# A Fourier filter and a gated MLP on one core: another order in the filter stage, its last tile split over two engines

## The chip, the cores and the metric

The kernel runs on one core of a Trainium2 chip. Five engines work side by side: PE (matmuls), DVE and POOL (elementwise), ACT (activations and copies) and SP (here it issues transfers). The metric is the device time of one execution in microseconds. The kernel before has a median of 455.23 us over three runs (455.15 to 455.26).

## The reference, cut to what matters

`x` has 2048 rows of 512. Each row is normalised, the whole is taken through a 2-D Fourier transform, multiplied by a complex filter and transformed back; the result is added to `x`. Then a normalised copy goes through a gated MLP (512 to 1376 twice, GELU of one half times the other, back to 512) and is added again.

```python
def _A_ref(x, w_r, w_i):
    X = rfft2(x)                      # over 2048 rows and 512 columns
    return irfft2(X * (w_r + 1j * w_i), (S, D))

def _B_ref(x, w_gate, w_up, w_down):
    return (gelu(x @ w_gate) * (x @ w_up)) @ w_down

h = x + _A_ref(layernorm(x), A_w_r, A_w_i)
h2 = h + _B_ref(layernorm(h), B_w_gate, B_w_up, B_w_down)
```

All in float32.

## The kernel before, in words

The rows stand in 16 row blocks of 128 (index b), the 512 columns in four chunks of 128 or, in the Fourier domain, in 16 tiles (index t). Transforms are matmuls with tables of cosines. All results of a stage go back to one large tile in SBUF, `gh`. The eight banks of PSUM are the columns of `ps`.

The kernel has four stages.

1. *Transform over the rows* (to 32 us): per row block, statistics, folding on POOL, matmuls of line 288.
2. *The filter stage* (32 to 77 us), one pass over the 16 tiles t. Its order is written out by hand in the string `SECOND`, which is walked word by word; with `tc.manual_schedule` every engine gets its instructions in just that order. The words are:
   - `o3.0`: `over_d`, four matmuls of line 416 into two banks (the number behind the point is the first one), then two ACT copies into `dp` (line 420).
   - `f3`: `filtered`, two matmuls of line 427 into the two banks 4 and 5 (t even) or 6 and 7 (t odd); three products with the filter `wt` on DVE (lines 433, 434, 435) into `t1` and `t2`, which read these banks; the sum `z` on POOL (line 438) and a small addition of column 128 to column 0 (line 440). For the last tile, t = 15, sum and small addition are on DVE. `f` of tile t also issues on SP the load of the filter for tile t + 8 (line 202).
   - `b3`: `back`, four matmuls of line 448 that read `z` and fill bank t mod 2, then one ACT copy into `gh` (line 450).
   - `p3`: `patch_w`, a small ACT copy into the filter of tile t (line 453), which must come ahead of `f3`'s products and behind the load of this tile's filter.
   - `h`: one step in the preparation of the first and second weight tiles of the MLP ("raw tiles"): a rounded copy on ACT (line 93) and the remainder on POOL (line 94), and between the two tiles the transfer of the second (lines 131, 132) and four additions on POOL (lines 138 to 146).
3. *Transform back over the columns and rows, and the start of the MLP* (77 to about 131 us). Its order is the string `FIRST`. `U4.0` is `over_d_back` of row block 4 into bank 0: four matmuls of line 515, one for each chunk of columns, which read row block 4 of `gh` and so the back-transforms of all 16 tiles. `C4.0` copies the bank to a row on ACT (line 830), `V4.2` (DVE, line 838) and `X4` (POOL, line 866) unfold it, `M4.1` is the transform over the rows (PE, line 848), `H`, `G`, `I` the residual, `S`, `A`, `Q` statistics, and so on. `r0` to `r3` are the first four POOL steps on the third raw tile (`r0` is line 138), whose transfer is issued on SP ahead of `FIRST`.
4. *The MLP* (to the end), matmuls of lines 100 to 102 and 747.

A multiplication of float32 goes through PE in two passes, so four matmuls appear as eight in the trace. PE, ACT, DVE and POOL each work strictly in their own order: an instruction that waits holds all that stand behind it on its engine. SP's queue of transfers is in order too.

Of the kernel before, what the change touches and what calls it, by code (L numbers as in the profile page):

```python
# [20 lines left out]
P = 128  # L21
NB = 16
NT = 16
NF = 11
NQ = 260
# [6 lines left out]
BY_THEN = (8, 12, 9)  # L32

FIRST = """
U4.0 C4.0 r0 U0.1 C0.1 U1.2 U5.3 V4.2 X4 V0.3 C1.4 V1.0 C5.5 X0 M4.1 V5.1 X1 O4.0 X5 M0.2 H4 U2.3 O0.1 G4 I4
M5.1 C2.5 H0 V2.3 G0 S4 U7.2 M1.3 O5.0 A4 U6.0 I0 U3.4 X2 H5 C7.1 S0 O1.1 A0 H1 M2.1 C6.0 Q0 C3.5 E0.5 N0 G5
U12.3 R01 V7.4 I5 T01.2 G1 I1 V6.3 S5 X7 A5 R00 T00 S1 O2.1 M7.0 X6 s0.0 A1 a0 Q1 l0 V3.1 E1.6 c0 d0 f0 b0 U8.4
U9.7 N1 e0.1 m0 g0 H2 h0 R10 k0 T10 R11 H7 n0 T11.1 X3 a1 s1.2 b1 c1 i0 d1 j0 l1 M3.2 C8 S7 g0aP0 o0 M6.4 e1.0
h1 f1 U14.5 k1 C12 i1 m1 n1 O6.0 g1 g0ac1 U15.3 H3 j1 S3 C15 o1 A3 g0aP1 C9 A7 g0aP2 Q3 C14 G2 H6 g0ac2 E3.7 I2
N3 g0aP3 G6 U10.4 g0aP4 R31 S2 I6 R30 g0ad1 g0ac3 A2 S6 T31.5 A6 T30 s3.6 g0aP5 g1aP0 a3 Q2 E2.6 g0ady c3 C10  # L40
g0aP6 d3 b3 N2 f3 r1 g1ac1 g3 e3.4 K9.5 g1aP1 R20 r2 h3 g1aP2 i3 g1ad1 g1aP3 k3 R21 j3 T20 T21.7 g1ac2 a2 b2
s2.8 c2 g1aP4 g1ac3 l3 g1aP5 g0bP0 K12.4 d2 m3 g0ad2 n3 f2 g1ady g1aP6 e2.7 g2 g0bP1 o3 k2 l2 m2 g0bc1 h2 n2 i2
# [4 lines left out]
"""  # L47

SECOND = """
p0 p1 p2 h o0.0 h o1.6 o2.2 f0 o3.0 f1 p3 o4.2 f2 p4 h o5.0 o6.2 h f3 o7.0 h h p5 h f4 o8.2 p6 f5 b0 p7 b1 f6 o9.2 h h  # L50
h f7 p8 p9 b2 b3 o10.2 p10 f8 b4 h p11 o11.2 p12 f9 b5 o12.2 h h f10 b6 f11 o13.2 p13 b7 f12 h h o14.2 b8 f13 p14 o15.2
h f14 p15 b9 b10 h f15 b11 h b12 b13 b14 b15
"""
AHEAD = 8

# [2 lines left out]
def kernel(  # L58
# [47 lines left out]
    ps = ctx.enter_context(tc.tile_pool(name="ps", bufs=1, space=PSUM)).tile([P, 8, 512], F32, name="ps")  # L106
# [55 lines left out]
    with (  # L162
# [245 lines left out]
        w2 = ctx2.enter_context(tc.tile_pool(name="w2", bufs=2, reuse_waits="tile"))  # L408
        dps, zs = {}, {}
# [12 lines left out]
        def filtered(t):  # L422
            dp, wt = dps.pop(t), wts.pop(t)
            px = ps[:, 4 + 2 * (t % 2) : 6 + 2 * (t % 2), :NQ]
            for g in range(2):
                r = dp[:, g].rearrange("p e q -> p (e q)")
                pe.matmul(px[:, g], cfs[:, min(t, 1), g], r, start=True, stop=True)  # L427

            t1 = w2.tile([P, 2, NQ], F32, name="t1", bufs=3)
            t2 = w2.tile([P, 2, NQ], F32, name="t2", bufs=3)  # L430
            z = w2.tile([P, 2, NQ], F32, name="z", bufs=7)
            re, im = slice(0, 64), slice(64, P)
            dve.tensor_tensor(t1, px, wt[:, 0], op=ALU.mult)
            dve.scalar_tensor_tensor(t2[re], px[im], -1.0, wt[im, 1], op0=ALU.mult, op1=ALU.mult)
            dve.tensor_tensor(t2[im], px[re], wt[re, 1], op=ALU.mult)

            eng = dve if t == NT - 1 else pool
            eng.tensor_tensor(z, t1, t2, op=ALU.add)
            zs[t] = z
            eng.tensor_tensor(z[:, :, 0], z[:, :, 0], z[:, :, 128], op=ALU.add)  # L440

        def back(t):
            z = zs.pop(t)
            pg = ps[:, t % 2].rearrange("p (c g n) -> p c g n", c=4, g=2)
            for e in range(2):
                for g in range(2):
                    o, zg = pg[:, 2 * e : 2 * e + 2, g], z[:, g, 130 * e : 130 * e + P]
                    pe.matmul(o, zg, cis[:, min(t, 1), g], start=True, stop=True)  # L448
            ghv = gh.rearrange("p b (c t k) -> p t c b k", c=8, k=4)[:, t]
            act.activation(ghv, ps[:, t % 2].rearrange("p (c b k) -> p c b k", c=8, k=4), AF.Copy)  # L450

        def patch_w(t):
            act.activation(wts[t][:, :, :, 0:129:128], wh[:, t], AF.Copy)
# [2 lines left out]
        with tc.manual_schedule(engines={et.PE, et.Activation, et.DVE, et.Pool}):  # L456
# [50 lines left out]
        dve.bn_aggr(mv2[:, b], bn)  # L507
        yield

    def over_d_back(b, bank):  # L510

        g = gh[:, b].rearrange("p (c k) -> p c k", c=4)
        pv = ps[:, bank].rearrange("p (e s n) -> p e s n", e=2, s=2)
        for c in range(4):
            pe.matmul(pv[:, c // 2, (c + c // 2) % 2], g[:, c], dis[:, c], start=True, stop=True)  # L515

    def norm_scales(b, n):
# [269 lines left out]
    do = {}  # L787
# [25 lines left out]

    def whole(b):

        pv = sv = v = py = od = None
        xt, by_pe = sources[b], b in BY_PE

        def parts(a):
            return a.rearrange("p (e s n) -> p e s n", e=2, s=2)  # L820

        def back(k):
            nonlocal pv
            pv = ps[:, k]
            over_d_back(b, k)

        def keep(k):
            nonlocal sv
            sv = parts(rows[k])
            act.activation(rows[k], pv, AF.Copy)  # L830

        def unfold(k):
            nonlocal v
            v = rows[k]
            if b in BY_POOL:
                pool.tensor_tensor(parts(v)[:, :, 0], sv[:, :, 0], sv[:, :, 1], op=ALU.add)
            else:
                dve.tensor_tensor(parts(v)[:, :, 0], parts(pv)[:, :, 0], sv[:, :, 1], op=ALU.add)

        def back_s(k):  # L840
            nonlocal py
            py = ps[:, k].rearrange("p (e n) -> p e n", e=2)
            if by_pe:
                for e, m in enumerate((mis[:, b], nis[:, BY_PE.index(b)])):
                    pe.matmul(py[:, e], mis[:, b], v[:, :256], start=True, stop=False)  # L845
                    pe.matmul(py[:, e], m, v[:, 256:], start=False, stop=True)
            else:
                pe.matmul(ps[:, k], mis[:, b], v, start=True, stop=True)  # L848
# [12 lines left out]
        def unfold2(e, op):  # L861
            x2, h2 = (a.rearrange("p (e n) -> p e n", e=2) for a in (xt, gh[:, b]))
            return lambda: pool.tensor_tensor(h2[:, e], x2[:, e], od, op=op)

        do[f"U{b}"], do[f"C{b}"], do[f"V{b}"], do[f"M{b}"] = back, keep, unfold, back_s
        do[f"X{b}"] = lambda: pool.tensor_tensor(parts(v)[:, :, 1], sv[:, :, 0], sv[:, :, 1], op=ALU.subtract)
# [47 lines left out]
    for b in range(8):  # L914
        whole(b)
# [240 lines left out]
```

## Time and profile before

| What | us |
|---|---|
| Median of three runs | 455.23 |
| Profiled execution | 455.09 |
| Its span, first to last instruction | 453.3 |
| PE busy in the span | 438.1 |
| POOL busy | 276.0 |
| DVE busy | 276.7 |
| ACT busy | 206.5 |
| Filter stage on PE, first matmul of line 416 to first of line 515 | 32.40 to 76.89 |

The profile is of one execution. Its times run from the start of the span. "Idle before" is the time for which an engine had nothing to do ahead of an instruction, with the instruction that ended it. A group in the order of time has its start, its length and how many instructions it holds; matmuls overlap, so a group's row ends a little later than the next one starts.

### The profile page before, as it was taken

How to read it: one execution, taken by the hardware profiler on the slowest of the kernel's cores; microseconds unless marked ns; L12 is line 12 of the kernel's file. 1: busy time of each engine (PE TensorE's matmuls, PEld its weight loads, DVE VectorE, ACT ScalarE, POOL GpSimd, SP SyncE). 2: the span in 40 equal slices, each digit the busy share in tenths (PEclk: the TensorE clock that was granted, in tenths of full speed). 3: DMA queues.
4: the chain of work that ended last, by engine and by line, in shares of the span. 5: the costliest groups of instructions: out<-in, count | busy, mean ns of one | idle time of the engine just before them, and what ended most of it. 6: DMA issues, size and time to landing. Idle time of an engine off the chain costs nothing.

```text
span 453.3 us, 6435 instructions
## 1 busy us (share of the span) xinstructions
PE 438.1 (97%) x2289; PEld 371.2 (82%) x2289; DVE 276.7 (61%) x513; ACT 206.5 (46%) x433; POOL 276.0 (61%) x305
## 2 busy tenths in 40 slices
PE   3999999999999999999999999999999999999996
PEld 3999998788878777877888888888888888888875
DVE  5957886797565766358734579266655355635453
ACT  4979776688741243034322775242243024303420
POOL 6985996968869578738662643165566546663210
PEclk9999999999999999999999999999999999999999
DMA  8994805200032022112210213121122102210013
GB/s 293 392 395 145 274 11 185 95 25 1 25 116 74 31 83 93 48 46 71 69 46 25 70 40 123 48 93 46 26 69 71 46 24 71 69 46 25 23 70 117
DMA packets 21168, 41.05 MB, mean 91 GB/s; under 512 B 2064, under 2 KB 7696, under 8 KB 21008
## 3 DMA queue, kind: packets, MB, share of 16 engines
q1 hardware_dynamic: 20992, 40.51, 25.9%
q8 instruction: 18, 0.29, 0.3%
q10 hardware_dynamic: 144, 0.13, 0.1%
q14 instruction: 14, 0.11, 0.1%
HBM read 36.44 MB, written 4.19 MB: 90 GB/s over the span
## 4 chain that ended last, share of the span: by engine, by line
PE 93%; DVE 3%; ACT 2%; DMA 1%; issue 1%; SPq 0%; DVEq 0%
PE ps L747 26%; PE ps L100 15%; PE ps L102 15%; PE ps L101 15%; PE ps L288 5%; PE ps L416 3%; PE ps L515 3%; PE ps L427 3%; PE ps L448 2%; PE ps L848 1%; PE ps L956 1%; DMA gh<-in_x 1%; PE ps L554 1%; PE ps L548 1%; PE ps L845 0%
## 5 line engine op out<-in xcount | busy, mean ns | idle before, releaser
L100 PE MATMUL ps<-cb,gu 128*128 128x512 f32 (+1 forms) x336 | 127.8, 380 | 2.0 <-ACT s L651 1.6
L747 PE MATMUL ps<-wd,a 128*128 128x512 f32 (+1 forms) x537 | 125.9, 387 | 0.2 <-DVE gh L750 0.2
L102 PE MATMUL ps<-cb,gu 128*128 128x512 f32 (+1 forms) x336 | 124.8, 372 | 0.0
L101 PE MATMUL ps<-cb,gu 128*128 128x512 f32 (+1 forms) x336 | 124.8, 371 | 0.0
L747 PEld LDWEIGHTS ps<-wd,a 128*128 128x128 f32 x537 | 99.3, 188 | 22.0 <-DVE gh L957 1.0
L156 POOL TENSOR_TENSOR gu<-raw,gu 128x768 fp32r<-128x768 f32 (+1 forms) x54 | 78.3, 1479 | 39.8 <-DVE gu L153 36.0
L651 ACT ACTIVATE s<-ps 128x512 f32<-128x512 f32 (+1 forms) x72 | 40.4, 561 | 133.7 <-PE ps L102 133.4
L100 PEld LDWEIGHTS ps<-cb,gu 128*128 128x128 f32 x336 | 63.2, 188 | 14.9 <-ACT s L651 2.2
L101 PEld LDWEIGHTS ps<-cb,gu 128*128 128x128 f32 x336 | 63.3, 188 | 11.7 <-issue 1.0
L102 PEld LDWEIGHTS ps<-cb,gu 128*128 128x128 f32 x336 | 63.2, 188 | 11.0
L753 DVE TENSOR_TENSOR gh<-ps,gh 128x512 f32<-128x512 f32 x48 | 33.1, 691 | 53.4 <-PE ps L747 53.3
L496 POOL TENSOR_TENSOR wd<-wdr,wd 128x512 fp32r<-128x512 f32 x22 | 28.5, 1295 | 50.9 <-ACT wd L494 50.9
L660 DVE TENSOR_TENSOR ps<-ps,s 128x512 f32<-128x512 f32 (+1 forms) x48 | 31.0, 650 | 24.8 <-PE ps L102 22.5
L666 ACT ACTIVATE a<-ps 128x512 fp32r<-128x512 f32 (+1 forms) x48 | 26.9, 561 | 38.9 <-DVE ps L660 38.6
L138 POOL TENSOR_TENSOR raw<-raw 128x256 f32<-128x256 f32 x20 | 14.7, 737 | 38.3 <-DMA raw<-in_wgu 37.2
L673 DVE TENSOR_TENSOR a<-ps,a 128x512 fp32r<-128x512 f32 (+1 forms) x48 | 30.8, 641 | 11.5 <-ACT a L666 9.8
L654 DVE TENSOR_TENSOR s<-ps,s 128x512 f32<-128x512 f32 (+1 forms) x48 | 30.9, 643 | 10.3 <-PE ps L102 8.7
L657 ACT ACTIVATE s<-s 128x512 f32<-128x512 f32 (+1 forms) x48 | 28.2, 592 | 18.4 <-DVE s L654 18.4
L654 DVE TENSOR_TENSOR ps<-ps,s 128x512 f32<-128x512 f32 (+1 forms) x24 | 15.7, 654 | 27.7 <-ACT s L651 27.7
L288 PE MATMUL ps<-ms,pn 128*128 128x128 f32 x120 | 17.4, 295 | 7.6 <-ACT ms L256 7.4
L288 PEld LDWEIGHTS ps<-ms,pn 128*128 128x128 f32 x120 | 16.0, 209 | 8.0 <-POOL pn L263 7.4
L153 DVE CAST gu<-raw 128x1792 fp32r<-128x1792 f32 x18 | 19.6, 1091 | 4.5 <-PE ps L101 2.9
(124 smaller groups left out, 609.6 us busy)
## 6 DMA issues: line engine op xcount, KB each, us to landing
raw<-in_wgu SPq DMA_DIRECT2D x40, 256.0 KB, 3.1
wt<-in_w SPq DMA_DIRECT2D x16, 520.0 KB, 5.5
wdr<-in_wd SPq DMA_DIRECT2D x22, 256.0 KB, 2.7
out<-gh SPq DMA_DIRECT2D x15, 256.0 KB, 2.0
gh<-in_x SPq DMA_DIRECT2D x7, 512.0 KB, 8.0
row<-in_x SPq DMA_DIRECT2D x12, 256.0 KB, 3.0
mis<-in_mi SPq DMA_DIRECT2D x1, 1024.0 KB, 10.8
a<-in_x SPq DMA_DIRECT2D x4, 256.0 KB, 4.1
```

Of the source, the lines that this page charges most:

```text
L100: pe.matmul(o, lh, rh, start=(i == 0 and not onto), stop=False, skip_group_check=True)
L101: pe.matmul(o, lh, rl, start=False, stop=False, skip_group_check=True)
L102: last = pe.matmul(o, ll, rh, start=False, stop=(i == n - 1), skip_group_check=True)
L156: pooled["lo"] = pool.tensor_tensor(r[:, 1, m], t[:, m], r[:, 0, m].bitcast(F32), op=ALU.subtract)
L288: pe.matmul(pt[:, c], o, mc, start=(z == 0), stop=(z == len(parts[b][c]) - 1))
L496: pool.tensor_tensor(r[:, 1], t, r[:, 0].bitcast(F32), op=ALU.subtract)
L651: return lambda: act.activation(to, a, AF.Copy)
L654: return lambda: dve.tensor_tensor(to, a, b, op=ALU.add)
L660: return lambda: dve.tensor_tensor(u, u, g, op=ALU.mult)
L673: dve.tensor_tensor(a[:, 1], u, a[:, 0].bitcast(F32), op=ALU.subtract)
L747: pe.matmul(o, parts_of[tiles.index((q, f))][:, ha, i // 4, r], wds[f][:, hw, c], start=start, stop=stop)
L753: dve.tensor_tensor(gh[:, b, c], o, gh[:, b, c], op=ALU.add)
```

## The change

Five things change.

The string `SECOND` is another: the `h` and `p` steps, `o`, `f` and `b` stand in a different sequence. On PE, near the start of the filter stage, `f3` now comes ahead of `o6`. PE before (line 416 is `over_d`, 427 `filtered`, 448 or now 454 `back`):

```order
29 L416 MATMUL ps<-dfs,ts 128x130 x12
30 L427 MATMUL ps<-dp,cfs 128x260 x2
31 L416 MATMUL ps<-dfs,ts 128x130 x4
32 L427 MATMUL ps<-dp,cfs 128x260 x2
33 L416 MATMUL ps<-dfs,ts 128x130 x4
34 L427 MATMUL ps<-dp,cfs 128x260 x2
35 L416 MATMUL ps<-dfs,ts 128x130 x8
36 L427 MATMUL ps<-dp,cfs 128x260 x2
```

PE in the changed kernel, the same place:

```order
29 L416 MATMUL ps<-dfs,ts 128x130 x12
30 L427 MATMUL ps<-dp,cfs 128x260 x2
31 L416 MATMUL ps<-dfs,ts 128x130 x4
32 L427 MATMUL ps<-dp,cfs 128x260 x2
33 L416 MATMUL ps<-dfs,ts 128x130 x4
34 L427 MATMUL ps<-dp,cfs 128x260 x2
35 L416 MATMUL ps<-dfs,ts 128x130 x4
36 L427 MATMUL ps<-dp,cfs 128x260 x2
37 L416 MATMUL ps<-dfs,ts 128x130 x8
38 L427 MATMUL ps<-dp,cfs 128x260 x2
```

Row 36 of the new order is f3; it stood behind two `over_d` (x8) and stands behind one.

At the end of the filter stage PE had one `back` fewer behind f15. Before (f14, two backs, f15, five backs, then stage 3):

```order
62 L416 MATMUL ps<-dfs,ts 128x130 x4
63 L427 MATMUL ps<-dp,cfs 128x260 x2
64 L448 MATMUL ps<-cis,z 128x2x64 x8
65 L427 MATMUL ps<-dp,cfs 128x260 x2
66 L448 MATMUL ps<-cis,z 128x2x64 x20
67 L515 MATMUL ps<-dis,gh 128x128 x16
```

In the changed kernel:

```order
62 L416 MATMUL ps<-dfs,ts 128x130 x4
63 L427 MATMUL ps<-dp,cfs 128x260 x2
64 L454 MATMUL ps<-cis,z 128x2x64 x8
65 L427 MATMUL ps<-dp,cfs 128x260 x2
66 L454 MATMUL ps<-cis,z 128x2x64 x24
67 L524 MATMUL ps<-dis,gh 128x128 x16
```

f15 is followed by six backs (x24) where it was followed by five. The sixteen matmuls of the last row are U4, U0, U1 and U5 before, and u4, u0, w4, w0, U1 and U5 now.

POOL at the same place, with the third raw tile's first step (line 138) ahead of the unfolding of row block 4 (line 866). Before:

```order
72 L438 TENSOR_TENSOR z_814<-t1_812,t2_813 128x520
73 L440 TENSOR_TENSOR z_814<-z_814 128x2
74 L94 TENSOR_TENSOR gu_82<-raw_575,gu_82 128x256 x2
75 L138 TENSOR_TENSOR raw_913<-raw_913 128x256
76 L866 TENSOR_TENSOR row_889<-row_887 128x2x128
77 L866 TENSOR_TENSOR row_890<-row_888 128x2x128
```

In the changed kernel:

```order
73 L443 TENSOR_TENSOR z_812<-t1_810,t2_811 128x520
74 L444 TENSOR_TENSOR z_812<-z_812 128x2
75 L441 TENSOR_TENSOR z_832<-t1_830,t2_831 128x2x130
76 L94 TENSOR_TENSOR gu_82<-raw_574,gu_82 128x256
77 L881 TENSOR_TENSOR row_891<-row_889 128x2x128
78 L881 TENSOR_TENSOR row_892<-row_890 128x2x128
```

POOL has its half of the last z (line 441) ahead of the last split, and the raw step is gone from here; it now stands behind `C15` in `FIRST`.

The other four: `z` has 14 buffers instead of 7. The last `z` is added by halves of its columns, 0 to 129 on DVE and 130 to 259 on POOL. The last `back` fills two banks, columns by the first half of `z` into bank 1 and by the second into bank 3; ACT copies the first to `gh` and DVE the second. Row blocks 4 and 0 are begun by halves of d: `u4` and `u0` are the two chunks that the first copy fills, `w4` and `w0` the other two. And `r0` moves as said. On SP, the transfer of the second raw tile now stands one place earlier, ahead of the load of the filter for tile 13. Line numbers behind line 440 are 6 to 15 higher in the changed kernel.

The diff (of the two strings only the lines with a moved word that the text speaks of):

```diff
 FIRST = """
-U4.0 C4.0 r0 U0.1 C0.1 U1.2 U5.3 V4.2 X4 V0.3 C1.4 V1.0 C5.5 X0 M4.1 V5.1 X1 O4.0 X5 M0.2 H4 U2.3 O0.1 G4 I4
+u4.0 u0.1 w4 C4.0 w0 C0.1 U1.2 U5.3 V4.2 X4 V0.3 C1.4 V1.0 C5.5 X0 M4.1 V5.1 X1 O4.0 X5 M0.2 H4 U2.3 O0.1 G4 I4
...
-h1 f1 U14.5 k1 C12 i1 m1 n1 O6.0 g1 g0ac1 U15.3 H3 j1 S3 C15 o1 A3 g0aP1 C9 A7 g0aP2 Q3 C14 G2 H6 g0ac2 E3.7 I2
+h1 f1 U14.5 k1 C12 i1 m1 n1 O6.0 g1 g0ac1 U15.3 H3 j1 S3 C15 r0 o1 A3 g0aP1 C9 A7 g0aP2 Q3 C14 G2 H6 g0ac2 E3.7 I2
...
 SECOND = """
-p0 p1 p2 h o0.0 h o1.6 o2.2 f0 o3.0 f1 p3 o4.2 f2 p4 h o5.0 o6.2 h f3 o7.0 h h p5 h f4 o8.2 p6 f5 b0 p7 b1 f6 o9.2 h h
...
-h f14 p15 b9 b10 h f15 b11 h b12 b13 b14 b15
+h p0 h o0.6 o1.0 h o2.2 p1 h f0 o3.0 f1 p2 o4.2 f2 o5.0 p3 h f3 o6.2 p4 o7.0 h h p5 f4 p6 o8.2 p7 p8 f5 b0 b1 f6 h h
+o9.2 p9 h h p10 b2 f7 o10.2 f8 b3 o11.2 b4 p11 h h h f9 o12.2 p12 f10 h p13 b5 f11 o13.2 b6 p14 f12 p15 o14.2 h b7 f13
+h o15.2 f14 b8 b9 f15 b10 b11 h b12 b13 b14 b15
...
-            z = w2.tile([P, 2, NQ], F32, name="z", bufs=7)
+            z = w2.tile([P, 2, NQ], F32, name="z", bufs=14)
...
+            zs[t] = z
+            first = slice(0, NQ)
+            if t == NT - 1:
+                first, second = slice(0, 130), slice(130, NQ)
+                pool.tensor_tensor(z[:, :, second], t1[:, :, second], t2[:, :, second], op=ALU.add)
             eng = dve if t == NT - 1 else pool
-            eng.tensor_tensor(z, t1, t2, op=ALU.add)
-            zs[t] = z
+            eng.tensor_tensor(z[:, :, first], t1[:, :, first], t2[:, :, first], op=ALU.add)
             eng.tensor_tensor(z[:, :, 0], z[:, :, 0], z[:, :, 128], op=ALU.add)
 
         def back(t):
-            z = zs.pop(t)
-            pg = ps[:, t % 2].rearrange("p (c g n) -> p c g n", c=4, g=2)
+            z, last = zs.pop(t), t == NT - 1
+            ghv = gh.rearrange("p b (c t k) -> p t c b k", c=8, k=4)[:, t]
             for e in range(2):
+                pt = ps[:, 3 if last and e else t % 2]
+                pg = pt.rearrange("p (c g n) -> p c g n", c=4, g=2)
                 for g in range(2):
                     o, zg = pg[:, 2 * e : 2 * e + 2, g], z[:, g, 130 * e : 130 * e + P]
                     pe.matmul(o, zg, cis[:, min(t, 1), g], start=True, stop=True)
-            ghv = gh.rearrange("p b (c t k) -> p t c b k", c=8, k=4)[:, t]
-            act.activation(ghv, ps[:, t % 2].rearrange("p (c b k) -> p c b k", c=8, k=4), AF.Copy)
+                c = slice(4 * e, 4 * e + 4) if last else slice(0, 8)
+                if last and e:
+                    dve.tensor_copy(ghv[:, c], pt.rearrange("p (c b k) -> p c b k", c=8, k=4)[:, c])
+                elif last or e:
+                    act.activation(ghv[:, c], pt.rearrange("p (c b k) -> p c b k", c=8, k=4)[:, c], AF.Copy)
...
-    def over_d_back(b, bank):
+    def over_d_back(b, bank, cs=range(4)):
...
-        for c in range(4):
+        for c in cs:
...
+        def back_first(k):
+            nonlocal pv, bank
+            pv, bank = ps[:, k], k
+            over_d_back(b, k, (0, 1))
...
+        do[f"u{b}"], do[f"w{b}"] = back_first, lambda: over_d_back(b, bank, (2, 3))
```

More of the change, by code (lines that the diff above doesn't have):

```diff
@@ L49 @@
 SECOND = """
-p0 p1 p2 h o0.0 h o1.6 o2.2 f0 o3.0 f1 p3 o4.2 f2 p4 h o5.0 o6.2 h f3 o7.0 h h p5 h f4 o8.2 p6 f5 b0 p7 b1 f6 o9.2 h h
-h f7 p8 p9 b2 b3 o10.2 p10 f8 b4 h p11 o11.2 p12 f9 b5 o12.2 h h f10 b6 f11 o13.2 p13 b7 f12 h h o14.2 b8 f13 p14 o15.2
-h f14 p15 b9 b10 h f15 b11 h b12 b13 b14 b15
+h p0 h o0.6 o1.0 h o2.2 p1 h f0 o3.0 f1 p2 o4.2 f2 o5.0 p3 h f3 o6.2 p4 o7.0 h h p5 f4 p6 o8.2 p7 p8 f5 b0 b1 f6 h h
+o9.2 p9 h h p10 b2 f7 o10.2 f8 b3 o11.2 b4 p11 h h h f9 o12.2 p12 f10 h p13 b5 f11 o13.2 b6 p14 f12 p15 o14.2 h b7 f13
+h o15.2 f14 b8 b9 f15 b10 b11 h b12 b13 b14 b15
 """
@@ L814, in whole @@
     def whole(b):
-        pv = sv = v = py = od = None
+        pv = sv = v = py = od = bank = None
         xt, by_pe = sources[b], b in BY_PE
```

## The prediction

> **What bounds the kernel now.** I read four views in this order: the page's totals, the stretches with the busy time of each engine, the waits of PE, and the order of time around the one place where PE waits.
>
> The totals:
>
> ```profile
> span 453.3 us, 6435 instructions
> ...
> PE 438.1 (97%) x2289; PEld 371.2 (82%) x2289; DVE 276.7 (61%) x513; ACT 206.5 (46%) x433; POOL 276.0 (61%) x305
> ```
>
> PE is busy 97% of the span. The other engines count only where PE waits for them. The stretches (start:end, length, then busy time and instructions of PE, PEld, DVE, ACT, POOL, then PE's granted clock, 1.00) say where that is around the filter stage:
>
> ```profile
> 32.40:70.20 37.80, 37.80 (x278) 35.82 (x279) 30.61 (x44) 31.98 (x72) 30.47 (x43) 1.00 0.46 156
> 70.20:77.70 7.50, 6.38 (x51) 5.89 (x50) 4.46 (x7) 4.49 (x10) 4.55 (x7) 1.00 0.43 143
> ...
> 131.50:437.00 305.50, 305.37 (x1346) 249.47 (x1345) 172.46 (x284) 106.73 (x196) 172.34 (x171) 1.00 0.17 57
> ```
>
> From 32.40 to 70.20 PE has no idle time, so a new order of the same matmuls cannot shorten that piece; it can only open gaps in it. From 131.5 to 437 it has 0.13 us. In the 7.5 us between, at the end of the filter stage, it is idle 1.12 us. The waits of PE name the two causes (total, times, longest):
>
> ```profile
> PE ps L100 <- ACT s L651: 1.6, 3, 0.7
> ...
> PE ps L515 <- ACT gh L450: 0.7, 1, 0.7
> PE ps L448 <- DVE z L440: 0.4, 1, 0.4
> ```
>
> The last two are this place, the first lies behind 110 us. In order of time the place reads (start, length, engine, instruction, in brackets the idle time before):
>
> ```profile
> 45.93 1.95 PE L448 MATMUL ps<-cis,z 128*128 128x128 f32 x16
> 47.71 1.04 PE L427 MATMUL ps<-dp,cfs 128*128 128x260 f32 x4
> ...
> 69.91 1.04 PE L427 MATMUL ps<-dp,cfs 128*128 128x260 f32 x4
> 70.79 3.85 PE L448 MATMUL ps<-cis,z 128*128 128x128 f32 x32
> ...
> 71.16 0.70 DVE L433 TENSOR_TENSOR t<-ps,wt 128x520 f32<-128x520 f32 x1 [0.16 <-ACT gu L93]
> ...
> 71.88 0.60 ACT L450 ACTIVATE gh<-ps 128x512 f32<-128x512 f32 x1 [0.47 <-PE ps L448]
> 72.38 0.41 ACT L93 ACTIVATE gu<-raw 128x256 fp32r<-128x256 f32 x1
> 72.59 0.69 DVE L435 TENSOR_TENSOR t<-ps,wt 64x520 f32<-64x520 f32 x1
> ...
> 73.04 1.87 POOL L94 TENSOR_TENSOR gu<-raw,gu 128x256 fp32r<-128x256 f32 x2
> 73.31 1.01 DVE L438 TENSOR_TENSOR z<-t,t 128x520 f32<-128x520 f32 x1
> ...
> 74.36 0.57 DVE L440 TENSOR_TENSOR z<-z 128x2 f32<-128x2 f32 x1
> 74.68 0.60 ACT L450 ACTIVATE gh<-ps 128x512 f32<-128x512 f32 x1 [0.30 <-PE ps L448]
> ...
> 75.08 1.13 PE L448 MATMUL ps<-cis,z 128*128 128x128 f32 x8 [0.43 <-DVE z L440]
> ...
> 76.24 0.60 ACT L450 ACTIVATE gh<-ps 128x512 f32<-128x512 f32 x1 [0.96 <-PE ps L448]
> ...
> 76.89 1.16 PE L515 MATMUL ps<-dis,gh 128*128 128x128 f32 x8 [0.69 <-ACT gh L450]
> ```
>
> A back-transform of one tile (b, eight passes of L448) issues in 0.89 us: two start at 45.93 and the next work at 47.71. Five of them, b11 to b15, would take 5 x 0.89 = 4.45 us. They take 76.89 - 70.79 = 6.10 us. So the end of the stage loses **1.65 us**. That is the two idle times, 1.12 us, twice the 0.17 us by which the next group normally starts before the last one has drained (70.79 + 3.85 is 74.64, the issue would have been free near 74.48), and about 0.1 us slower issue behind each wait (1.13 and 1.16 us for eight where 1.05 is usual).
>
> **The change, part by part.**
>
> *The order of the filter stage.* No matmul is added or removed. f15 (the row at 69.91) now has five backs behind it ahead of b15, where it had four. It therefore starts 0.89 us sooner, at 69.02. From the end of its row DVE followed by 71.16 - 70.95 = 0.21 us; now that is 70.27, and three products with the row lengths above end 2.12 us later, near 72.4. The price is an early wait. f3 moves ahead of o6, to the place of o6 near 40.58, and must find its pair of banks released by the third product of f1:
>
> ```profile
> 39.64 1.99 PE L416 MATMUL ps<-dfs,ts 128*128 128x130 f32 x16
> 41.47 1.04 PE L427 MATMUL ps<-dp,cfs 128*128 128x260 f32 x4
> ...
> 45.02 1.07 PE L427 MATMUL ps<-dp,cfs 128*128 128x260 f32 x4
> ...
> 36.32 0.70 DVE L433 TENSOR_TENSOR t<-ps,wt 128x520 f32<-128x520 f32 x1 [6.87 <-issue]
> ...
> 39.90 0.69 DVE L435 TENSOR_TENSOR t<-ps,wt 64x520 f32<-64x520 f32 x1
> ...
> 44.20 0.69 DVE L435 TENSOR_TENSOR t<-ps,wt 64x520 f32<-64x520 f32 x1
> ```
>
> The product of f1 (39.90) ends at 40.59, so f3 waits some 0.06 us and pays 0.1 us for the slower issue: +0.16 us, with 0 and 0.4 as ends. f5 stays where it stood (45.02 in the old order) and needs the product that ends at 44.89, the last row: no wait.
>
> *The last z on two engines.* DVE adds 260 of 520 columns, POOL the rest. The nearest row for the DVE half is an addition of two SBUF operands of 256 columns; for the POOL half a row of the same size is the first of the second pair:
>
> ```profile
> 28.62 0.42 DVE L275 TENSOR_TENSOR us<-pn 128x256 f32<-128x256 f32 x1
> ...
> 98.92 0.73 POOL L573 TENSOR_TENSOR cb<-s,cb 128x256 fp32r<-128x256 f32 x1 [1.52 <-ACT cb L570]
> ```
>
> The DVE half lies between 0.42 and 1.01 us (the whole addition beside POOL). With L440's 0.57 us and two steps of 0.04 the first half is ready between 73.4 and 74.1 us. b15 can issue at 74.48 at the earliest, plus f3's 0.16: it is covered by 0.5 us or more, and the wait of 0.43 us goes. POOL's half must be there 0.45 us later. POOL's old queue shows L94 twice from 73.04; now the half stands ahead of one of them. A start at 72.9 and 0.73 us, or 0.94 as L94 took beside DVE, gives 73.6 to 73.8: covered by 1.3 us.
>
> Here a rule speaks against the change. The Trainium skill, "SBUF — State Buffer", section "Who interferes with whom", says that a DVE instruction with two SBUF inputs contends with a GpSimd instruction that reads SBUF, and that the one that comes second blocks for the whole instruction. The old rows look like it: 1.01 us for DVE and 0.94 each for POOL at 73 us. If DVE's half had to stand behind all of POOL's, the first half would be ready at 72.4 + 0.73 + 0.42 + 0.57 + 0.12 = 74.2 us, still ahead of 74.5, so by this rule the sum stays as it is.
>
> *The last back in two halves, copied by ACT and DVE; u and w.* Before, all eight passes, then one ACT copy of 0.60 us, then L515. Now the first four passes (0.45 us) fill one bank, ACT copies half of it while the other four run, and u4, u0 read only that half. Count from b15's start T: the fourth pass has drained at T + 0.61 (0.33 to its start, 0.28 for one pass). ACT is still at b14's copy until about T + 0.70 (that copy started 74.68 - 74.48 = 0.20 behind the free issue, and 71.88 to 72.38 shows that a copy frees ACT after 0.50). The half copy takes as long as the form of 256 columns:
>
> ```profile
> L93 ACT ACTIVATE gu<-raw 128x256 fp32r<-128x256 f32 x14 | 5.4, 408 | 0.1
> ```
>
> T + 1.11, and 0.05 to reach PE: u4 starts at T + 1.16 where PE would be free at T + 0.89. What is left is 0.27 us plus 0.1 for slow issue, **0.37 us**; the ends are 0.1 (ACT free in time) and 0.6 (the copy takes the full 0.60). The DVE copy of the other half starts with the last drain near T + 1.1, and with 0.42 to 0.60 us is done by T + 1.7; w4 comes behind u4 and u0, at T + 1.16 + 0.89 = T + 2.05. Covered by 0.3.
>
> C4 now stands behind u4, u0 and w4 instead of U4 alone. Its followers are POOL's X4 and PE's M4 (L848). In the old order POOL had the raw step r0 ahead of X4:
>
> ```profile
> 79.14 0.73 POOL L138 TENSOR_TENSOR raw<-raw 128x256 f32<-128x256 f32 x1 [4.23 <-DMA raw<-in_wgu]
> 79.82 2.80 POOL L866 TENSOR_TENSOR row<-row 128x256 f32<-128x256 f32 x4
> ...
> 80.61 1.99 PE L848 MATMUL ps<-row,mis 128*128 128x512 f32 x4
> ...
> 82.59 0.89 PE ps L515 x8
> ```
>
> X4 ended at 80.5 and M4 began at 80.61, hardly later than PE could. With r0 gone X4 starts with C4's end. C4 starts when w4 has drained, 3 x 0.45 - 0.11 + 0.28 + 0.04 = 1.56 us behind u4's start, takes 0.60, X4 0.73, the two steps 0.13: 3.0 us. M4's turn comes after four row blocks, 4 x 0.89 = 3.56 (last row). This fits by 0.5; with r0 still there (0.73) it would not. I take 0, with 0.2 as the bad end.
>
> *r0 moved back.* It now stands behind C15, ahead of the L573 at 98.92 above, where POOL was idle 1.52 us; its 0.73 us and its one read of a tile that has long landed fit. The two transfers of the third raw tile stay where they stand in SP's queue. Cost 0.
>
> *14 z buffers.* POOL no longer waits for a buffer. No PE wait in the old trace comes from that; gain 0.
>
> *The raw tiles' other steps* come sooner, and SP's load of the second raw tile now stands ahead of the load for tile 13, which is queued behind its wait for POOL:
>
> ```profile
> 49.68 0.38 SPq L131 DMA_DIRECT2D raw<-in_wgu  x1
> ...
> 51.41 2.48 SPq L202 DMA_DIRECT2D wt<-in_w  x2
> ...
> wt<-in_w SPq DMA_DIRECT2D x16, 520.0 KB, 5.5
> ```
>
> POOL's last step on the first raw tile follows its z3, whose inputs come at 44.89 (row above): 1.5 us for z3 and 1.4 for two splits give 47.8, two issues of 0.4, the load 5.5 us: tile 13 lands near 54.2. p13 stands on ACT ahead of o13's copy, near 58. Cost 0, with 4 us in hand.
>
> **Sum.** -1.65 + 0.37 + 0.16 = -1.12 us. Behind it PE, ACT, DVE and POOL all run on what PE releases, and the transfers of x and of the third raw tile are released by this same stretch, so the shift should last to the end. The profiled execution had 455.09 us, 1.79 beyond its span; it would have 453.97. The median of the runs is 0.14 higher, 455.23, so I predict **454.1 us**.
>
> **Rivals.**
>
> *DVE's pace opens gaps in the full stretch.* Between two f with one unit between them PE needs 0.88 + 0.89 = 1.77 us, DVE 3 x 0.715 = 2.15. Three places (f9 to f10, f10 to f11, f13 to f14) are like that; each can cost 0.38 us if DVE is then behind. For it: DVE is busy 30.6 of 37.8 us there. Against it, in the new order: DVE's nine products f0 to f8 end at 36.32 + 9 x 2.15 = 55.7 if nothing holds it; f9 stands twelve units behind f5, at 45.02 + 12 x 0.89 = 55.7, its products run from 56.95 to 59.1; f11, the first to ask for that pair of banks, comes at 55.7 + 2 x 1.77 = 59.24. It is close, 0.1 us. All three together give 1.14 us back: 455.2, no change. Chance 0.16.
>
> *The shift is lost behind 100 us.* PE's 1.6 us of waits for ACT (L651) would grow if ACT there hung on a transfer with a fixed time. Nothing in the waits names one. It would end at about 455.2. Chance 0.07.
>
> *Slower: tile 13 late.* If POOL finishes the first raw tile after about 52 us instead of 47.8, p13 holds ACT, o13's copy and then PE. Each us beyond costs PE one us; from 53.1 on the kernel is slower, and with POOL at 55, some 3 us late on PE, it ends at 456.1. Against it: POOL has gaps there. Chance 0.06. Other losses of that size, such as M4 or the second half late, together 0.05.
>
> *The end goes wholly.* If ACT is free in time and f3 does not wait, 0.1 stays: 453.7. Chance 0.06; the forecast itself 0.60.
>
> **How the numbers follow.** About 0.2%, 0.9 us, is what a measurement tells from no change, so 454.3 is the border, and the forecast lies 0.2 beyond it. Of its 0.60 I give 0.54 to faster and 0.06 to no difference (a residue at its upper end). With the 0.06 above faster has 0.60; no difference 0.06 + 0.16 + 0.07 = 0.29; slower 0.11. The range starts at 453.7 and reaches to 455.2, which takes in the rivals of no change.
>
> **What the profile will show.** PE's wait for z at the last back gone; the wait for ACT ahead of the first row block down from 0.7 to about 0.1 to 0.3 us; that block starting near 75.8 instead of 76.89; no DVE or POOL releaser for M4; p13 without a DMA wait; and all later PE times earlier by one same amount. I am wrong if the stretch 32.4 to 70 shows PE idle by more than 0.3 us, or the offset shrinks behind 100 us.

## The result and the profile after

The changed kernel has a median of 454.13 us over eight runs (453.98 to 454.49). The kernel before, run beside it on the same chip, has 455.19 us (455.06 to 456.76). The ratio is 0.9976 with a 95% interval of 0.9966 to 0.9985: faster by about 1.06 us. The forecast was 454.1 us. The profiled execution took 454.05 us.

The totals of the changed kernel:

```profile
span 452.3 us, 6433 instructions
...
PE 437.8 (97%) x2289; PEld 371.1 (82%) x2289; DVE 277.1 (61%) x514; ACT 205.6 (45%) x433; POOL 276.5 (61%) x306
```

The work is nearly the same: the span has lost 1.0 us, while PE is busy for 437.8 us where it was 438.1, ACT for 0.9 us less and DVE and POOL for 0.4 and 0.5 us more. The stretches of the changed kernel, with the same columns as in the prediction:

```profile
32.40:70.20 37.80, 37.80 (x275) 35.71 (x276) 31.39 (x45) 31.98 (x74) 31.51 (x44) 1.00 0.49 164
70.20:76.60 6.40, 6.33 (x55) 6.05 (x54) 3.67 (x6) 3.62 (x8) 3.96 (x7) 1.00 0.31 104
...
131.50:436.00 304.50, 304.33 (x1343) 249.09 (x1341) 172.75 (x283) 105.91 (x195) 171.86 (x171) 1.00 0.17 56
```

The full stretch is still full, although DVE and POOL have more to do in it. At the end of the filter stage PE is idle 0.07 us where it was 1.12. The waits of PE in the changed kernel (total, times, longest):

```profile
PE ps L288 <- ACT ms L256: 7.8, 2, 7.3
PE ps L100 <- ACT s L660: 1.6, 3, 0.6
PE ps L416 <- ACT ts L293: 0.7, 1, 0.7
PE ps L100 <- DVE ps L663: 0.3, 1, 0.3
PE ps L756 <- DVE gh L759: 0.2, 1, 0.2
```

The two rows of the kernel before for the end of the filter stage, 0.7 us for `gh` and 0.4 us for `z`, are gone, and no row for that place has come instead. The end of the stage in order of time, changed kernel:

```profile
69.06 1.04 PE L427 MATMUL ps<-dp,cfs 128*128 128x260 f32 x4
...
69.94 5.77 PE L454 MATMUL ps<-cis,z 128*128 128x128 f32 x48
...
70.31 0.70 DVE L433 TENSOR_TENSOR t<-ps,wt 128x520 f32<-128x520 f32 x1 [0.17 <-POOL z L443]
...
72.46 0.43 DVE L443 TENSOR_TENSOR z<-t,t 128x260 f32<-128x260 f32 x1
72.55 0.40 POOL L444 TENSOR_TENSOR z<-z 128x2 f32<-128x2 f32 x1
72.90 0.73 POOL L441 TENSOR_TENSOR z<-t,t 128x260 f32<-128x260 f32 x1
72.93 0.73 DVE L444 TENSOR_TENSOR z<-z 128x2 f32<-128x2 f32 x1
...
74.34 0.33 SPq L131 DMA_DIRECT2D raw<-in_wgu  x1
74.72 0.43 SPq L132 DMA_DIRECT2D raw<-in_wgu  x1
74.85 0.87 ACT L459 ACTIVATE gh<-ps 128x512 f32<-128x512 f32 x2 [0.42 <-PE ps L454]
75.26 2.49 SPq L792 DMA_DIRECT2D a<-in_x  x4
...
75.78 3.84 PE L524 MATMUL ps<-dis,gh 128*128 128x128 f32 x32
...
79.45 1.88 PE L862 MATMUL ps<-row,mis 128*128 128x512 f32 x4
```

L454 is the old L448, L524 the old L515, L862 the old L848. The 48 passes of b10 to b15 stand in one group, without a gap that the view shows, and the first row block follows 75.78 - 69.94 = 5.84 us after their start. Six backs at 0.89 us would take 5.34, so the end of the stage now loses **0.50 us**, where it lost 1.65.

Did the gain last to the end? The stage starts between 32.10 and 32.70 us in the profiles of this document, so distances are compared, not times. The rows for it are the first matmul group of the stage, the first matmul of the MLP and the last group of matmuls. Kernel before, order of time:

```profile
32.40 2.95 PE L416 MATMUL ps<-dfs,ts 128*128 128x130 f32 x24 [0.69 <-ACT ts L293]
...
96.64 0.47 PE L100 MATMUL ps<-cb,gu 128*128 128x256 f32 x1
...
437.08 12.68 PE L747 MATMUL ps<-wd,a 128*128 128x512 f32 x63 [0.17 <-DVE gh L750]
```

Changed kernel, order of time:

```profile
32.30 2.95 PE L416 MATMUL ps<-dfs,ts 128*128 128x130 f32 x24 [0.69 <-ACT ts L293]
...
95.57 0.47 PE L100 MATMUL ps<-cb,gu 128*128 128x256 f32 x1
...
436.05 12.68 PE L756 MATMUL ps<-wd,a 128*128 128x512 f32 x63 [0.17 <-DVE gh L759]
```

From the start of the stage, the first row block comes after 44.49 us before and 43.48 now (1.01 less), the MLP after 64.24 and 63.27 (0.97 less), the last group after 404.68 and 403.75 (0.93 less). What the end of the filter stage gained is kept almost whole.

### The profile page after: what moved, and what is told of

Read it like the earlier page. It is cut to its first block, busy times and chain, and to the rows that moved or that the text cites. A ratio compares the mean times of both kernels' runs of the same rounds, so it can differ in the third digit from the quotient of the medians.

```text
span 452.3 us, 6433 instructions
## 1 busy us (share of the span) xinstructions
PE 437.8 (97%) x2289; PEld 371.1 (82%) x2289; DVE 277.1 (61%) x514; ACT 205.6 (45%) x433; POOL 276.5 (61%) x306
## 4 chain that ended last, share of the span: by engine, by line
PE 90%; DVE 3%; ACT 2%; DMA 2%; POOL 1%; issue 1%; SPq 0%; POOLq 0%; DVEq 0%
PE ps L756 26%; PE ps L100 15%; PE ps L102 14%; PE ps L101 14%; PE ps L288 4%; PE ps L416 3%; PE ps L427 3%; PE ps L454 3%; PE ps L524 3%; PE ps L862 1%; PE ps L971 1%; DMA gh<-in_x 1%; POOL gu L156 1%; PE ps L563 1%; DMA raw<-in_wgu 1%; PE ps L557 1%
## 5 line engine op out<-in xcount | busy, mean ns | idle before, releaser
L100 PE MATMUL ps<-cb,gu 128*128 128x512 f32 (+1 forms) x336 | 127.9, 381 | 2.0 <-ACT s L660 1.6
L100 PEld LDWEIGHTS ps<-cb,gu 128*128 128x128 f32 x336 | 63.3, 188 | 14.9 <-ACT s L660 2.2
```

The costliest lines, as they stand in the source:

```text
L100: pe.matmul(o, lh, rh, start=(i == 0 and not onto), stop=False, skip_group_check=True)
```

## The experiments

The theory: the gain is the end of the filter stage, as the prediction summed it, and the order and the new tail (the sum on two engines, the halves of the last back, u and w) each carry a part. The rivals: one of the two carries all of it; or a part costed at nothing carries some.

Each group of kernels ran beside the kernel before on one chip; its median there was 455.17 us for the first four runs (order alone, without the order, r0, interleaved), 455.58 for the next four (whole row blocks, buffers, `z` on DVE, f3) and 455.39 for the last four (the two with x first, each with its kernel without it). The changed kernel itself was in none of these groups, so its median and theirs compare only by way of the kernel before. Below, "stage" is the distance from the first L416 group to the first row block, "to MLP" the distance from there to the first L100, both from the profiled execution.

| Kernel | median us (lowest to highest) | ratio to before, 95% | stage | to MLP |
|---|---|---|---|---|
| before | 455.19 | | 44.49 | 19.75 |
| after | 454.13 (453.98 to 454.49) | 0.9976 (0.9966 to 0.9985) | 43.48 | 19.79 |
| order alone | 454.71 (454.40 to 455.90) | 0.9993 (0.9985 to 1.0002) | 44.09 | 19.60 |
| without the order | 454.42 (454.13 to 456.93) | 0.9987 (0.9977 to 0.9998) | 43.25 | 20.41 |
| r0 at its old place | 455.44 (454.37 to 455.83) | 1.0001 (0.9993 to 1.0010) | 43.47 | 20.98 |
| row blocks whole | 454.28 (454.05 to 454.57) | 0.9965 (0.9950 to 0.9980) | 43.47 | 19.88 |
| 7 z buffers | 454.28 (454.13 to 454.48) | 0.9965 (0.9951 to 0.9980) | 43.47 | 19.79 |
| last z on DVE alone | 454.24 (454.03 to 454.58) | 0.9968 (0.9953 to 0.9983) | 43.47 | 19.79 |
| f3 behind o6 | 454.52 (454.38 to 454.91) | 0.9970 (0.9954 to 0.9985) | 43.83 | 19.81 |
| last two backs interleaved | 453.76 (453.48 to 455.14) | 0.9972 (0.9962 to 0.9981) | 43.24 | 19.51 |
| without the order, x first | 453.44 (453.24 to 453.77) | 0.9955 (0.9943 to 0.9967) | 43.26 | 19.60 |
| interleaved, x first | 453.46 (453.29 to 453.57) | 0.9955 (0.9942 to 0.9968) | 43.23 | 19.50 |

### The order alone

The kernel before with the new string `SECOND`, nothing else.

> The kernel before with the new string SECOND alone (one issue order for all engines in the filter stage; last z whole on DVE, last back whole, ACT copy whole, row blocks whole, r0 in its old place, 7 z buffers). My theory: the order removes the wait of PE for the last z (f15 starts 0.89 us sooner, z ready near 74.2 and needed near 74.4), and leaves the wait of 0.69 us for ACT ahead of L515, for 0.10 us paid at f3. The first L515 then starts near 76.2 to 76.3 against 76.89, total gain 0.6 us, about 454.6. Rival 1, the order carries all of the change: L515 near 75.8 and 454.1. Rival 2, the order is worth nothing since another wait takes over: L515 stays near 76.9, 455.2.

Measured: 454.71 us. Order of time, order alone:

```profile
69.87 5.76 PE L448 MATMUL ps<-cis,z 128*128 128x128 f32 x48
...
76.32 3.84 PE L515 MATMUL ps<-dis,gh 128*128 128x128 f32 x32 [0.69 <-ACT gh L450]
```

Six backs take 76.32 - 69.87 = 6.45 us, 1.11 more than 5.34. The wait for `z` is gone, the wait of 0.69 us for `gh` is still there in full. In the stage of this profile the order alone is worth 44.49 - 44.09 = 0.40 us; by the medians the gain is 0.46 us, where 0.6 was expected, and the interval of the ratio takes in no change. Between the theory and its second rival, then, the trace decides and not the time.

### Everything but the order

```diff
-h p0 h o0.6 o1.0 h o2.2 p1 h f0 o3.0 f1 p2 o4.2 f2 o5.0 p3 h f3 o6.2 p4 ...
+p0 p1 p2 h o0.0 h o1.6 o2.2 f0 o3.0 f1 p3 o4.2 f2 p4 h o5.0 o6.2 h f3 o7.0 ...
...
```

> The changed kernel with the old string SECOND: the split of the last z and of the last back, the half row blocks, r0 moved and 14 buffers stay, the order of the filter stage is that of before. My theory: DVE ends the third product of tile 15 near 73.3 as before, the half sum (0.43) and the small addition (0.73) bring the first half to 74.5, so PE waits about 0.1 us there (0.43 before) and then as in the changed kernel about 0.5 us in all ahead of the row blocks; no wait at f3. First row block near 75.9, total 454.2 to 454.3, a gain of 0.9 to 1.0. If the order were needed for the gain (rival), the wait for z stays near 0.4 and the total is 454.5 or more. If this theory holds, the two parts together are worth much less than the sum of each alone.

Measured: 454.42 us, a little above the expected range, and with a wide spread, though the first row block comes sooner than expected (75.45 us, not 75.9). The stage is shorter than in the changed kernel, 43.25 against 43.48 us: in the stage the tail alone gains 1.24 us, more than both together (1.01). PE's waits have no row for `z` although f15 has only four backs ahead of b15. What the kernel loses, it loses later. Order of time, without the order:

```profile
70.59 5.00 PE L454 MATMUL ps<-cis,z 128*128 128x128 f32 x40
...
73.58 0.57 DVE L444 TENSOR_TENSOR z<-z 128x2 f32<-128x2 f32 x1
...
74.09 0.74 POOL L441 TENSOR_TENSOR z<-t,t 128x260 f32<-128x260 f32 x1
...
75.54 0.33 SPq L131 DMA_DIRECT2D raw<-in_wgu  x1
75.91 0.44 SPq L132 DMA_DIRECT2D raw<-in_wgu  x1
76.46 1.82 SPq L792 DMA_DIRECT2D a<-in_x  x4
...
81.58 1.41 DVE L873 SCALAR_TENSOR_TENSOR a<-a,mv,ps 128x512 f32<-128x512 f32 x2 [1.13 <-DMA a<-in_x]
...
82.47 1.10 PE L862 MATMUL ps<-row,mis 128*128 128x512 f32 x2 [0.57 <-DVE a L873]
```

The wait for `z` goes by little. DVE's half is ready at 74.15 us and POOL's at 74.83, and PE is through with the issue of all five backs at 70.59 + 5.00 - 0.17 = 75.42, of which the four passes on POOL's half need 0.45.

The third raw tile is issued when POOL has done its last split of the second one. In the old order that is at 75.54 us, 1.20 us later than in the changed kernel (74.34), and the four loads of `x` stand behind it on SP. The residual of row block 4 (`H4`, L873) then waits for `x`, and PE behind it.

### Without the order, x ahead of the raw tile

The reading above was put to the test by one more edit in that kernel: the loads of `x` come first on SP, the third raw tile behind them.

```diff
-        nc.sync.dma_start(sources[b], x3[:, b])
+        i = nc.sync.dma_start(sources[b], x3[:, b])
+        loaded = i if b == 5 else b and loaded
...
-    next(raw2)
+    with tc.issue_after(loaded.ins):
+        next(raw2)
```

> The kernel with the new end and the old order (e2_tail), but with the four x loads (tiles a) issued on SP ahead of the third raw tile's two transfers, which wait for POOL's last split. My theory: in e2_tail the residual at 81.6 us waits for x because SP stood at the raw tile until 75.5 us, 1.2 us later than in the changed kernel; with x first the wait of PE for DVE's a (0.6 us) goes, and the time falls by about 0.5 us, from 454.4 to 453.9 or 454.0. Rival: the x loads themselves are not released before 75.5 us (their space is read until then), or the wait comes from elsewhere on DVE: then the wait stays and the time is 454.4.

The kernel without it ran again beside it:

> The new end with the old order once more, beside e10_x_first on the same chip, since the difference between them is only some 0.5 us. Both theories: about 454.4 us, with PE's wait for DVE's a of 0.5 to 0.6 us.

Measured: **453.44 us** with x first, 454.55 (453.54 to 455.72) without it. Order of time, with x first:

```profile
74.86 1.75 SPq L792 DMA_DIRECT2D a<-in_x  x4
76.71 0.38 SPq L131 DMA_DIRECT2D raw<-in_wgu  x1
...
80.62 1.60 DVE L874 SCALAR_TENSOR_TENSOR a<-a,mv,ps 128x512 f32<-128x512 f32 x2 [0.15 <-ACT od L868]
```

The residual no longer waits for a transfer, and PE no longer for the residual. This confirms the cause; the gain is 1.1 us, twice what was expected. The spread suggests why: without the edit twelve executions lie 2.2 us apart, with it five lie 0.5 us apart. The second profile without it is of the fastest execution (453.54 us): there the way to the MLP is 19.73 us, the residual waits 0.45 us for `x`, and PE has no such wait. In the first profile the residual waited 1.13 us, PE 0.57, and the way was 20.41 us. So the time at which `x` lands changes from one execution to the next, and a profile of one execution shows one draw of it.

This kernel is 0.7 us faster than the changed one by their medians; the two ran in different groups, and their ratios to the kernel before are 0.9955 (0.9943 to 0.9967) and 0.9976 (0.9966 to 0.9985). So the new order is not needed for the gain. It has two effects: in the stage it costs 43.48 - 43.26 = 0.22 us once the new tail is there, and it lets POOL finish the second raw tile 1.2 us sooner, which brings the loads of `x` forward. The second can be had by four transfers in another place.

### r0 at its old place

```diff
-u4.0 u0.1 w4 C4.0 w0 C0.1 U1.2 ...
+u4.0 u0.1 w4 C4.0 r0 w0 C0.1 U1.2 ...
...
-... C15 r0 o1 ...
+... C15 o1 ...
```

> The changed kernel with r0 back behind C4, ahead of X4 on POOL. My theory: r0 waits for the third raw tile, whose transfer was issued 0.6 us sooner than in the kernel before, so r0 runs from about 78.55 to 79.28 instead of not at all, X4 ends near 80.0 and M4 (L862) starts near 80.05 instead of 79.45: 0.4 to 0.6 us of the gain is lost, 454.6. Rival, the move is worth nothing (M4 has 0.5 us in hand or the later work takes it up): M4 at 79.5 and 454.1.

Measured: 455.44 us, the same as the kernel before (ratio 1.0001). The loss is 1.3 us where 0.4 to 0.6 was expected. Order of time, r0 at its old place:

```profile
74.56 1.65 SPq L132 DMA_DIRECT2D raw<-in_wgu  x1
...
79.05 0.73 POOL L138 TENSOR_TENSOR raw<-raw 128x256 f32<-128x256 f32 x1 [4.89 <-DMA raw<-in_wgu]
79.74 2.78 POOL L881 TENSOR_TENSOR row<-row 128x256 f32<-128x256 f32 x4
...
80.51 1.98 PE L862 MATMUL ps<-row,mis 128*128 128x512 f32 x4 [0.92 <-POOL row L881]
```

The stage still gains its 1.02 us, and all of it is given back within 5 us: POOL stands at the raw tile until it lands, X4 comes behind, and the first L862 waits 0.92 us. That r0 at this place takes the gain is shown; how late the tile lands is not the same in all kernels. The order alone has r0 at its old place too, and there the tile lands 1.5 us sooner:

```profile
77.54 0.73 POOL L138 TENSOR_TENSOR raw<-raw 128x256 f32<-128x256 f32 x1 [3.86 <-DMA raw<-in_wgu]
```

X4 follows at 78.23 us, and PE has no wait at the first L848. The raw tile's first transfer was issued at 73.70 us there and at 74.19 here: POOL's last split, which releases it, comes later here because POOL adds its half of `z` ahead of it. The other 1.0 us of the 1.5 is open. The issue of L132 took 1.65 us here, against 0.43 in the changed kernel and in the order alone, and the times spread over 1.5 us, so the transfer may have had a bad draw; no run shows how much of the median that is.

### Three parts, one at a time

Three parts were undone one at a time in the changed kernel: the row blocks begun whole (`U4.0 C4.0 U0.1 C0.1` in place of the halves), seven buffers for `z`, and the last `z` added by DVE alone.

> The changed kernel with row blocks 4 and 0 begun whole again (U4, C4, U0, C0 instead of u4, u0, w4, C4, w0, C0), all else kept. U4's first two chunks read what ACT copied, its third what DVE copies until 76.23. My theory: PE comes to the third chunk at 75.78 + 0.45 = 76.23 and so waits about 0.05 us and pays 0.1 for the slower issue: the halves are worth 0.1 to 0.2 us, total 454.2 to 454.3. Rival, the halves carry the gain at this place: a wait of 0.4 us or more ahead of the third chunk, 454.5 or more. Rival, they are worth nothing, since C4 and X4 start sooner with U4 whole: 454.1.

> The changed kernel with 7 z buffers. My theory: no tile is more than six ahead of its back, so seven buffers hold it, no wait changes on PE, 454.1. Rival, POOL's sums wait for the backs that free their buffers and the last sums come late: a wait of PE for z appears, 454.4 or more.

> The changed kernel with the last z whole on DVE as before (the back and its copies still in halves). My theory: with the new order the whole sum (1.01 us beside POOL) and the small addition (0.57) end near 74.1, b15 needs it at 74.38, so nothing changes, 454.1; the split over two engines is covered twice. Rival, the shared port makes DVE's whole sum longer than in the kernel before, and PE waits at b15 by 0.2 to 0.5 us, 454.3 to 454.6.

Measured: 454.28, 454.28 and 454.24 us. All three stages are 43.47 us long, as in the changed kernel (43.48). With whole row blocks the way to the MLP is 0.09 us longer, too little to tell from the times; buffers and the split leave nothing to see. Given the new order, then, the sum on two engines is worth nothing; given the new tail, the order is worth nothing inside the stage. They are two cures for one wait of 0.43 us. That it is the sum on two engines that cures it in the tail is read from the rows (DVE's addition takes 0.43 us where it took 1.01); no run had that sum alone in the old order.

### f3 behind o6 again

```diff
-... p3 h f3 o6.2 p4 ...
+... p3 h o6.2 f3 p4 ...
```

> The changed kernel with f3 behind o6 again, where it stood before; all else kept. By the term of my prediction f3's early place costs 0.1 us (its row is 1.15 instead of 1.04 us long), so this would give 454.0. Rival: ACT has p3 and one split ahead of o6's copies in the new order, so o7, which needs the banks of o5, comes to PE before ACT has read them, and PE waits 0.2 to 0.4 us at o7 instead: 454.3 to 454.5.

Measured: 454.52 us, the stage 43.83 - 43.48 = 0.35 us longer. Order of time, f3 behind o6:

```profile
39.62 2.44 ACT L420 ACTIVATE dp<-ps 64x520 f32<-64x520 f32 x4
...
40.88 1.16 PE L416 MATMUL ps<-dfs,ts 128*128 128x130 f32 x8 [0.21 <-ACT dp L420]
```

Changed kernel, the same place:

```profile
40.55 1.15 PE L427 MATMUL ps<-dp,cfs 128*128 128x260 f32 x4
41.53 1.95 PE L416 MATMUL ps<-dfs,ts 128*128 128x130 f32 x16
```

In the new order o6 comes directly behind o5 if f3 does not stand between them, and it asks for the banks of o4. ACT comes to its copies of o4 and o5 only at 39.62, four of them in a row, and o6 waits for the first two. With f3 ahead of o6 they have time. So the theory, a gain of 0.1 us, was wrong. The rival had the loss right, but at the tile behind: it is o6 that waits for the banks of o4, not o7 for those of o5. f3 itself takes 41.53 - 40.55 = 0.98 us in the changed kernel, where 0.88 is usual.

### The last two backs interleaved

In the changed kernel ACT has to copy all of b14 before it can copy the first half of b15, and PE waits for both. Here b14 and b15 run as four half backs, the first halves of both ahead of the second ones, in four banks; ACT copies the first halves, DVE the second.

```diff
-... b12 b13 b14 b15
+... b12 b13 x14 x15 y14 y15
...
-def back(t):
+def back(t, es=(0, 1)):
...
-                pt = ps[:, 3 if last and e else t % 2]
+                pt = ps[:, ((0, 2), (4, 3))[t - NT + 2][e] if last else t % 2]
```

> The changed kernel with the last two backs interleaved: first halves of b14 and b15, then second halves, first halves copied by ACT and second halves by DVE, into four different banks. The 0.45 us of matmuls more between the first half of b15 and u4 should cover the rest of the copy chain. My theory: the 0.5 us that the changed kernel still loses between the last back (48 passes from 69.94, issue free at 75.28) and the first row block (75.78) goes but for 0.1; row block near 75.3 to 75.4, total 453.7. It needs the last z 0.45 us sooner (at 73.95; it was ready at 73.66). Rival 1: the wait is not that chain but a cost of changing the line, and 75.8 stays, 454.1. Rival 2: z comes too late by the added DVE work, and PE waits at b15 instead, 454.1 or more.

Measured: 453.76 us. Order of time, interleaved:

```profile
70.06 5.76 PE L454 MATMUL ps<-cis,z 128*128 128x128 f32 x48
...
75.66 3.74 PE L526 MATMUL ps<-dis,gh 128*128 128x128 f32 x32
```

5.60 us for six backs: 0.26 lost instead of 0.50. The half that is gone, 0.24 us, was PE's wait for ACT's copies. The half that is left is not that chain. ACT copies each back as soon as its last pass is through, so the starts of the copies show where PE comes late. Changed kernel, b10 to b13:

```profile
71.03 0.60 ACT L459 ACTIVATE gh<-ps 128x512 f32<-128x512 f32 x1 [0.78 <-PE ps L454]
71.93 0.60 ACT L459 ACTIVATE gh<-ps 128x512 f32<-128x512 f32 x1 [0.29 <-PE ps L454]
...
72.94 0.60 ACT L459 ACTIVATE gh<-ps 128x512 f32<-128x512 f32 x1
73.83 0.60 ACT L459 ACTIVATE gh<-ps 128x512 f32<-128x512 f32 x1 [0.30 <-PE ps L454]
```

The copy of b14 follows at 74.85. The steps are 0.90, 1.01, 0.89 and 1.02 us: b12 and b14 each come 0.12 us late. The interleaved kernel has the same step at b12 (72.05 to 73.06). The kernel before has it at b13:

```profile
72.77 0.60 ACT L450 ACTIVATE gh<-ps 128x512 f32<-128x512 f32 x1
73.79 0.60 ACT L450 ACTIVATE gh<-ps 128x512 f32<-128x512 f32 x1 [0.42 <-PE ps L448]
```

The views name no releaser for it. The time met the expected 453.7 us in part by luck: the stage gained 0.24 us where 0.4 was expected, and 0.28 us came behind it, on the way to the MLP (19.51 against 19.79), which the expectation did not speak of.

Then both improvements together, with this kernel again beside it on the same chip:

> The changed kernel with its last two backs interleaved by halves (e8_inter), and x ahead of the third raw tile. In e8_inter DVE's residual at 80.8 us still waited 0.24 us for x. If that is on PE's path, 453.5 to 453.6; if SP's order costs nothing once POOL is done by 74.3 us, 453.76 as before, within 0.1.

> The interleaved end once more, beside e11_inter_x_first on the same chip. Both theories: 453.7 to 453.8 us.

Measured: 453.46 us (453.29 to 453.57) with x first, 453.81 (453.61 to 454.02) without. x first is worth 0.35 us here. Together they are no faster than x first in the old order (453.44). By their medians both beat the changed kernel, and clearly the one before.

## Why the prediction was right

The time came out within 0.1 us of the forecast, and the mechanism is the one that was forecast. In the stage the sum is 0.11 us off (1.01 us measured, 1.12 forecast), by one term. What the prediction missed is how the parts hang on each other, and it was lucky with one of them, r0.

**The place.** It was the end of the filter stage and nothing else: PE's idle time there fell from 1.12 to 0.07 us, the stage is 1.01 us shorter, and 0.93 us of that is there at the last group of matmuls. Forecast: 1.12.

**The wait for z.** Forecast: f15 at 69.02, DVE's first product at 70.27, the first half of `z` ready at 73.4 to 74.1, POOL's half at 73.6 to 73.8. Measured: 69.06, 70.31, 72.93 + 0.73 = 73.66, and 72.90 + 0.73 = 73.63. But the prediction treated order and split as one cure. The runs show that the order alone and the tail alone each remove the wait.

**The residue.** The steps behind b15's start T held. The 48 passes free the issue at 69.94 + 5.77 - 0.17 = 75.54 us, so T is 75.54 - 0.89 = 74.65. ACT starts the copy of b14 at 74.85, T + 0.20 as forecast, and ends the half copy at 74.85 + 0.87 = 75.72; u4 starts at 75.78, T + 1.13, where T + 1.16 was forecast. The wait behind the free issue is 0.24 us against 0.27. The mis-sized step is T: "b15 can issue at 74.48 at the earliest, plus f3's 0.16" is 42.24 us behind the start of the stage, and b15 came at 74.65 - 32.30 = 42.35, 0.11 late. Backs in a row do not all issue in 0.89 us: one of the five in the kernel before and two of the six now take some 0.12 us more. The old trace had it already, since 70.79 + 4 x 0.89 is 74.35 and not 74.48. In the working of the 1.65 us this does not show, because the slow issue behind the second wait was counted in it, and that row (1.16) lies beyond 76.89, where the 1.65 end.

**f3.** Forecast 0.16 us, measured 0.1 at f3 itself. f15 comes 36.76 us behind the start of the stage where 69.02 - 32.40 = 36.62 would be free of any price, so all prices ahead of it are 0.14 us together. The size is right, but f3's place was costed against its old place in the old order. In the new order the old place costs 0.35 us more. The prediction did not look at what o5 and o6 in a row would ask of ACT there.

**r0.** Its move was costed at 0, and with that the sum came out. The sentence "with r0 still there (0.73) it would not" is right, but its working implies only 3.0 + 0.73 - 3.56 = 0.17 us. Put back, r0 takes the whole gain: 0.92 us at L862 in the profile, 1.3 us in the median. The step that was missing is r0's wait for its transfer, which is released by POOL's last split and not by PE. As far as this working goes, it is luck that the move was part of the change.

**The transfers.** "The transfers of x and of the third raw tile are released by this same stretch" is right, and it rests on the order: with the old one POOL is 1.2 us later with the second raw tile, and `x` behind it is late. So what the order costs in the stage it more than gives back on SP, which the prediction did not see.

**What was weighed against it.** DVE's half of `z` came first (72.46) and took 0.43 us, so it was not held up. Who came second was: POOL's addition of two columns, 0.20 us elsewhere, began at 72.55 and took 0.40, until 0.06 us after DVE's half had ended; DVE's addition of two columns began at 72.93, 0.03 behind POOL's half, and ended 0.03 behind it, after 0.73 us. By the rule of the Trainium skill, "SBUF — State Buffer", section "Who interferes with whom", a DVE instruction with two SBUF inputs and a POOL instruction that reads SBUF contend, and the one that comes second blocks; the trace agrees. The first half of `z` comes at 73.66 and not at 74.2, since POOL's half was second to DVE's, and at either time the backs cover it (T is 74.65).

**The rivals.** DVE's pace opened no gap: 37.80 of 37.80 us. The shift was not lost behind 100 us: of 1.01 us, 0.97 are there at the first L100 and 0.93 at the end. L862 has no DVE or POOL releaser. A late tile 13 would show as a wait of PE between 54 and 62 us, and there is none. What is open: from the first row block to the MLP the changed kernel needs 19.79 us, the kernels with x first 19.50 to 19.60, and without it the order alone 19.60 and the interleaved one 19.51. The place is near 88 us: from the start of L563 to the end of L557's issue the changed kernel needs 88.22 to 89.33, the one with x first in the old order 87.90 to 88.78, 0.23 us less. In the changed kernel the weight load of L557 waits 0.20 us for ACT there (L906, the normalised copy). Why ACT is later in that kernel no run took apart.

## What to carry to other kernels

Two edits that cure the same wait are worth it only once: cost each with the other in place, and look for what the second still takes (here 0.22 us in the stage). A step that waits for a transfer moves with what releases that transfer (here POOL's last split), not with the work around it: when only the work comes sooner, the wait grows, so such a step must leave the path or its transfer must be issued sooner. And when an order is changed, read SP's queue as closely as PE's: what stood behind the raw tile there was worth 1.1 us.

## What the runs showed of the hardware

Executions of one kernel can differ by 2 us through the time at which transfers land, and a profile of one execution does not show it. With the new tail in the old order, `x` behind the raw tile, twelve executions lay between 453.54 and 455.72 us; with `x` ahead of it five lay between 453.24 and 453.77. In the changed kernel, where `x` is behind the raw tile too but issued 1.2 us sooner, eight lay between 453.98 and 454.49. The issue on SP varies as well: the same L132 took 0.43 us in the changed kernel and 1.65 us in the kernel with r0 at its old place.

An addition of two columns on DVE that takes 0.57 us (kernel before, 74.36) or 0.73 us (changed kernel, 72.93) is mostly a wait for POOL: in both kernels it ends 0.02 to 0.03 us behind an instruction of POOL (L94 at 73.04 + 1.87, L441 at 72.90 + 0.73). Such a row is no price for that instruction when POOL does something else.
